# Second layer of a gated MLP by seven products of halves, with each chunk's operations recorded and issued from a written list

## The chip, the cores and the metric

The kernel runs on one core of one Trainium2 chip. The metric is the device time of one launch in microseconds (us). The core's engines work side by side, each through its own queue in order: PE (matrix products; PEld is its load of the stationary operand), DVE (vector), ACT (scalar), POOL (GpSimd) and SP, which here issues nearly all DMAs. SBUF is the on-chip memory, PSUM the accumulators that PE writes.

## The reference

Attention over 8 batches and 8 heads (512 local tokens with a window of 32 and 32 global tokens that see all), then a normalised gated MLP on all 4352 rows of 512 features. Only the MLP is touched by the change.

```python
rms = np.sqrt(np.mean(x * x, axis=-1, keepdims=True) + 1e-06)
xn = x / rms * rms_g
g = xn @ w_gate                      # first layer: 512 -> 1536, twice
silu = g * (1.0 / (1.0 + np.exp(-g)))
val = xn @ w_val
return (silu * val @ w_out)          # second layer: 1536 -> 512
```

## The kernel before

Rows are worked through in nine chunks: chunks 0 to 7 are the batches with 512 local tokens each, chunk 8 holds the 256 global tokens. While PE does the MLP of chunk c, the attention of chunks c+1 and c+2 goes on between its products.

Every fp32 number enters a product as two f16 parts, high and low, so one product is three: high by high, low by high, high by low.

*First layer.* Chunk 0 (order written out in `ORDER`), chunk 1 and chunk 8 use plain products (`moe_in`). Chunks 2 to 7 use `moe_pair`: two of the twelve feature tiles at a time, as a two by two block product done with seven products of halves (numbered 6, 1, 5, 7, 2, 3, 4) instead of eight. Each product is 12 matmuls with 256 moving columns. It needs sums of halves of the operands (`norm_halves` for the activations, `fold` once in chunk 1 for the weights, which go to a DRAM buffer `wd` and are fetched from it by `fetch` for every chunk) and sums of the results (`rest`). Behind it, in steps of a "tail", come the tanh on ACT, two multiplications on DVE (`gate`, `inner`), the high part as an ACT copy (`high`) and the low part as a subtraction, on POOL as a rule (`low`).

*Second layer.* `moe_block`: for each 128 tokens one PSUM bank, 12 feature tiles of three matmuls with 512 moving columns (the weights `wo`, held in SBUF); the stationary operand is the activation. So 36 matmuls a block, 144 a chunk of 512 tokens, 72 in chunk 8. The result is scaled by `inv_k` on ACT or DVE and stored by SP.

*Order.* After chunk 0 a loop over `work` issues one step (a product and its `rest`) at a time; behind each, `slot` issues those attention steps whose distances in steps from the ones they depend on have been kept, `norm_sums`, `norm_all`, `norm_halves` run at fixed distances from the chunk's end, `ch["tail", g]` at fixed places, and `feed` fetches the next weight tile from a list `ring`. Tiles of the pool `wf` (12 buffers of 512 KB) hold fetched weights `wt` and the fp32 sums `s`, `u`, `v`; the pools `wo` (7) and `h` (6) hold the second layer's weights and activations. PSUM banks: `po` twice, `pg`, `pv`, and four `pa` for attention.

The lines named below: L1106 is the first layer's matmul in `moe_pair`, L1264 the second layer's in `moe_block`, L1203 the plain first layer's, L706 and L660 attention's, L1160 `inner`, L157 a subtraction on POOL, L1138 the sum `s(6) + s(1)` on POOL, L1277 and L1275 the results on DVE and ACT, L1083 the fetch, L637 the division of the attention weights on POOL, L1054 and L1063 sums and high parts of `fold`.

Of the kernel before, what the change touches and what calls it, by code (L numbers as in the profile page):

```python
# [22 lines left out]
P = 128  # L23
# [40 lines left out]


@with_exitstack
def attention_moe_kernel(
# [29 lines left out]
    NORM[B - 1] = (17, 15, 12, 7)  # L97
    UNIT = {2: (0, 20), 3: (-26, 2, 12)}
    FOLD = (0, 6, 12, 18, 24, 30, 38, 46, 54)
    ST = 6  # L100
# [119 lines left out]
    def gain_bound():  # L220
        nc.vector.tensor_reduce(g2[:, 0:1], gp[0][:, 0:2], axis=AX.X, op=ALU.max)
        nc.vector.tensor_scalar(g2[:, 1:2], g2[:, 0:1], ginv, float(DM), ALU.mult, ALU.mult)
        nc.vector.tensor_scalar(x2, g2[:, 1:2], ginv, 2.0**-16, ALU.mult, ALU.mult)

# [189 lines left out]
    def out_scale():  # L414
        power(gp[0], 1, 15, k_o)
# [158 lines left out]
    def local_halves(c, b, hp, xt):  # L574
# [58 lines left out]
        def divide(x, bk):  # L633
            e = st["e", x, bk]
            r = st["sm"][:, 2, 8 * x + 4 * bk : 8 * x + 4 * bk + 4]
            nc.vector.reciprocal(r, r)  # L636
            nc.gpsimd.tensor_tensor(e, e, r.unsqueeze(2).to_broadcast([P, 4, P]), ALU.mult)  # L637

# [401 lines left out]
    ]  # L1040

    def fold(f):

        st = {}

        def sums():
            t = [
                pool.tile([P, 1152], F32, tag="st", bufs=ST, name=f"wq{f}")[:, :1024],
                pool.tile([P, 1024], F32, tag="wo", bufs=7, name=f"ws{f}"),
            ]  # L1050
            a, s = (x.rearrange("p (q n) -> p q n", q=4) for x in t)
            nc.vector.tensor_tensor(t[0], wf[f][:, 0, :], wf[f][:, 1, :], ALU.add)
            nc.vector.tensor_tensor(s[:, 1], a[:, 2], a[:, 3], ALU.add)
            nc.vector.tensor_tensor(s[:, 0], s[:, 1], a[:, 0], ALU.subtract)  # L1054
            nc.vector.tensor_tensor(s[:, 2], a[:, 0], a[:, 2], ALU.subtract)
            nc.vector.tensor_tensor(s[:, 3], a[:, 1], s[:, 0], ALU.subtract)
            st["s"] = s
            d = t[0].bitcast(F16)
            st["d"] = d.rearrange("p (q a n) -> p q a n", q=4, a=2)

        def high():
            d = st["d"]
            nc.scalar.copy(d[:, :, 0, :], st["s"])  # L1063
# [21 lines left out]

    def moe_pair(ch, g):

# [38 lines left out]
        def rest(p):  # L1126
# [5 lines left out]
            elif p == 1:  # L1132
                t = pool.tile([P, 1024], F32, tag="wf", bufs=NF, name=f"s1_{g}")
                st["s", 1], st["s", 5] = t[:, :512], t[:, 512:]
                nc.scalar.copy(s(1), st["ps", 1])  # L1135
            elif p == 5:
                nc.vector.tensor_tensor(s(5), st["ps", 5], s(1), ALU.add)  # L1137
                nc.gpsimd.tensor_tensor(s(6), s(6), s(1), ALU.add)  # L1138
            elif p == 7:
# [30 lines left out]
        def low(j, on="P"):  # L1170
            sub(on, st["h"][:, j, 1, :], st["t", j], st["h"][:, j, 0, :])

        ch["tail", g] = [
            lambda: gate(0),
            lambda: (gate(1), inner(0)),
            lambda: (inner(1), high(0)),
            lambda: (high(1), low(0)),
            lambda: low(1),
        ]
        if g == NF // 2 - 1:  # L1180
            ch["tail", g] = [
                lambda: (gate(0), gate(1)),
                lambda: (inner(0), inner(1), high(0)),
                lambda: (high(1), low(0)),
                lambda: low(1, "V"),
                lambda: None,
            ]
# [3 lines left out]
        ]  # L1191


    def moe_in(ch, w, f, n, ps, ks):
# [22 lines left out]

    def moe_f(ch, f, n, on):
        ps = {}
# [9 lines left out]
        def gate():  # L1229
# [6 lines left out]
            later(1, onto)  # L1236

        def inner():
            t = ps["t"]
# [12 lines left out]
            (lambda: half(1, 0), None),  # L1252
            (lambda: half(1, 1), inner),
        ]
# [105 lines left out]
    for c in range(NCH):  # L1360
# [3 lines left out]
        for i, un in enumerate(units):  # L1364
# [6 lines left out]
            for name, fn, pe, after in steps:  # L1371
                st = {"name": name, "fn": fn, "pe": pe, "c": c, "x": xi, "after": [], "at": None}
                st["from"] = (FIRST if c == EARLY else UNIT[len(units)])[i]
                for dep, gap in after:
# [11 lines left out]

    clock = [0]
    base = {}

# [14 lines left out]
    def slot(most, last):  # L1404

        done = 0
        for st in list(todo[:40]):
            if st["c"] > last:
                break
            if st["pe"] and done >= most:  # L1410
                continue
            if ready(st):
                issue(st)
                done += st["pe"]
# [24 lines left out]
    for name in ORDER.split():  # L1439
        job.pop(name)()  # L1440
    stores = [steps[3] for f, steps in folds.items() if f"J{f}" not in job]
    folds = {f: steps for f, steps in folds.items() if f"J{f}" in job}
    row = SL
    left = list(folds.values())
    ring = [(c, g, i) for c in range(EARLY, B) for g in range(NF // 2) for i in range(4)]
    ring += [(B, g, i) for g in range(NF // 2) for i in range(2)]

    def feed():
        if ring:
            fetch(*ring.pop(0))  # L1450

    base[1] = 0
    for c in range(1, NCH):
        n = width[c]
        ch = chunks[c]
        if EARLY <= c < B:
            work = [w for g in range(NF // 2) for w in moe_pair(ch, g)]
        else:
            work = [w for f in range(NF) for w in moe_f(ch, f, n, "P")]
        first = len(work)  # L1460
        work += [w for j in range(n // P) for w in moe_block(ch, j, row)]
        total = len(work)
        base[c + 1] = clock[0] + total
        gaps = NORM.get(c, NORMS)
# [3 lines left out]
        if c + 1 < NCH:  # L1468
# [5 lines left out]
            if not last:  # L1474
                for i, fns in norm_halves(chunks[c + 1], c + 1).items():
                    at[total - gaps[3] + i] = lambda fns=fns: [fn() for fn in fns]
        for k, (products, rest) in enumerate(work):
            products()
            if c + 1 < NCH:
                slot(1, c + 2)  # L1480
                if k == norm_at - 1:
                    assert not chunks[c + 1]["left"]
                    if last:
                        chunks[B]["x"] = [xg[:, kk, :] for kk in range(NK)]
                if k in at:
                    at[k]()
            if rest:
# [4 lines left out]
            if EARLY <= c < B and k >= 7 and k % 7 < 5 and k <= first + 4:  # L1492
                ch["tail", k // 7 - 1][k % 7]()
            if c == 1:
                if k == 1:
# [6 lines left out]
                if 42 <= k < 50:  # L1502
                    feed()
            elif c < B and k < first and k % 7 in (1, 3, 5, 6):
                feed()
            elif c == B - 1 and first <= k < first + 8:
                feed()
        row += n


# [124 lines left out]
```

## Time and profile before

| | |
|---|---|
| median of three runs | 928.01 us (926.51 to 928.34) |
| the profiled execution's own time | 924.96 us |
| its span, first to last instruction | 922.7 us |
| PE busy | 890.3 us, 96% |
| DVE busy | 634.3 us, 69% |
| ACT busy | 495.6 us, 54% |
| POOL busy | 253.5 us, 27% |
| moved by DMA | 173.39 MB, q1 at 56% of 16 engines |

The span is what the trace covers; the execution's own time is 2.3 us longer. Busy time of PE is the union of its matmuls, whose ends are modelled; since matmuls overlap in the array, the pace of a stream is read from a stretch of the chain (so many matmuls in so many us), and not from the duration of one.

### The profile page before, as it was taken

Reading aid. Unit: us, or ns where it says so; the run is one execution under the profiler, and the core shown is the slowest. Engines: PE = TensorE matmul, PEld = TensorE weight load, DVE = VectorE, ACT = ScalarE, POOL = GpSimd, SP = SyncE. Lnnn points to the kernel's source line nnn. Section 1 sums busy time; section 2 is a strip of 40 time slices with the busy share of each in tenths; the row PEclk is TensorE's granted clock in tenths of the full one; section 3 lists DMA queues with packets and bytes.
Section 4 is the critical chain, followed back from the end, with each engine's and each line's share of the span. In section 5 each row is a group of like instructions: output and inputs, shape, how many; then the busy total and the mean of one; then the engine's idle time right before and its main releaser. Section 6 shows DMA issues by size and latency. Waiting matters only on the chain.

```text
span 922.7 us, 26018 instructions
## 1 busy us (share of the span) xinstructions
PE 890.3 (96%) x10836; PEld 608.4 (66%) x10836; DVE 634.3 (69%) x1603; ACT 495.6 (54%) x1232; POOL 253.5 (27%) x219
## 2 busy tenths in 40 slices
PE   5699989999999999999999999999999999999998
PEld 4444446545447885688658874788568865886584
DVE  6999998887796578468765678457846874664331
ACT  6989996545444564357345545356435732553130
POOL 0000000142423252335333353225233431332020
PEclk9799999999999999999999999999999999999999
DMA  9983515686557863495519671776349522796000
GB/s 346 403 305 97 189 47 184 210 258 209 181 189 212 273 202 133 141 297 184 188 48 305 207 246 37 211 262 201 135 139 295 185 93 93 247 273 231 35 1 23
DMA packets 83493, 173.39 MB, mean 188 GB/s; under 512 B 6704, under 2 KB 25392, under 8 KB 83376
## 3 DMA queue, kind: packets, MB, share of 16 engines
q1 hardware_dynamic: 82944, 171.40, 56.0%
q8 instruction: 85, 1.39, 0.6%
q10 hardware_dynamic: 432, 0.33, 0.1%
q14 instruction: 32, 0.26, 0.1%
HBM read 150.21 MB, written 21.50 MB: 186 GB/s over the span
## 4 chain that ended last, share of the span: by engine, by line
PE 84%; DVE 1%; ACT 1%; issue 0%; DVEq 0%
PE pq L1106 36%; PE po L1264 25%; PE p L1203 9%; PE po L1331 3%; PE a L706 3%; PE s L660 3%; PE ga L836 1%; PE gs L779 1%; PE gt L822 1%; ACT e L622 1%; PE t L518 0%; PE s L474 0%; PE a L532 0%; DVE e L488 0%; ACT wq L295 0%
## 5 line engine op out<-in xcount | busy, mean ns | idle before, releaser
L1106 PEld LDWEIGHTS <-wt 128*128 128x128 f16 x3024 | 292.6, 98 | 41.1 <-issue 4.8
L1264 PE MATMUL po<-wo,h 128*128 128x512 f16 x1080 | 236.2, 379 | 0.0
L1106 PE MATMUL pq<-xh,wt 128*128 128x256 f16 x1152 | 204.5, 273 | 0.1
L1264 PEld LDWEIGHTS <-h 128*128 128x128 f16 x1080 | 105.2, 98 | 123.9 <-issue 1.0
L1106 PE MATMUL pq<-xl,wt 128*128 128x256 f16 x576 | 157.1, 273 | 0.7 <-issue 0.7
L1106 PE MATMUL pq<-ht,wt 128*128 128x256 f16 x1296 | 155.4, 273 | 0.0
L637 POOL TENSOR_TENSOR e<-e,sm 128x512 f32<-128x512 f32 x48 | 49.9, 1040 | 291.0 <-DVE sm L636 287.9
L157 POOL TENSOR_TENSOR h<-t,h 128x512 f16<-128x512 f32 (+1 forms) x90 | 102.5, 1146 | 93.1 <-ACT h L1246 52.4
L1203 PE MATMUL p<-xh,wf 128*128 128x512 f16 x384 | 117.6, 379 | 3.4 <-DVE t L1300 1.5
L1203 PEld LDWEIGHTS <-wf 128*128 128x128 f16 x576 | 55.3, 98 | 71.1 <-issue 4.9
L1138 POOL TENSOR_TENSOR s<-s,s 128x512 f32<-128x512 f32 x36 | 47.9, 1331 | 183.3 <-ACT s L1135 111.5
L622 ACT ACTIVATE e<-e,sm 128x128 f32<-128x128 f32 x192 | 75.2, 393 | 37.9 <-DVE sm L608 37.8
L1168 ACT CAST h<-t 128x512 f16<-128x512 f32 x72 | 44.4, 616 | 58.9 <-DVE t L1160 58.3
L1203 PE MATMUL p<-xl,wf 128*128 128x512 f16 x192 | 72.8, 379 | 0.3 <-DVE xl L902 0.3
L1160 DVE SCALAR_TENSOR_TENSOR t<-t,c_h,v 128x512 f32<-128x512 f32 x72 | 71.6, 1001 | 0.0
L1149 ACT ACTIVATE t<-u,half_inv 128x512 f32<-128x512 f32 x72 | 48.0, 714 | 36.9 <-DVE u L1124 28.5
L1124 DVE TENSOR_TENSOR v<-pq,s 128x512 f32<-128x512 f32 x72 | 49.6, 689 | 23.6 <-PE pq L1106 22.8
L1137 DVE TENSOR_TENSOR s<-pq,s 128x512 f32<-128x512 f32 x36 | 24.9, 691 | 46.9 <-PE pq L1106 40.5
L1156 DVE SCALAR_TENSOR_TENSOR t<-t,u 128x512 f32<-128x512 f32 x72 | 47.5, 688 | 1.0 <-ACT t L1149 1.0
L1124 DVE TENSOR_TENSOR u<-pq,s 128x512 f32<-128x512 f32 x36 | 24.9, 691 | 33.6 <-PE pq L1106 25.5
L608 DVE CUSTOM_DVE_ANT_0 e<-s,maskb 128x128 f32<-128x128 f32 x192 | 45.8, 278 | 2.0 <-PE s L660 2.0
L1131 ACT COPY s<-pq 128x512 f32<-128x512 f32 x36 | 21.0, 583 | 46.6 <-PE pq L1106 46.5
(346 smaller groups left out, 1275.5 us busy)
## 6 DMA issues: line engine op xcount, KB each, us to landing
wt<-wd SPq DMA_DIRECT2D x120, 512.0 KB, 4.7
wr<-in_w_in_dram SPq DMA_DIRECT2D x24, 512.0 KB, 8.8
k<-in_qkb_dram SPq DMA_DIRECT2D x24, 448.0 KB, 6.1
gkq<-in_gkq_dram SPq DMA_DIRECT2D x16, 576.0 KB, 6.3
wt<-wd SPq DMA_DIRECT2D x36, 256.0 KB, 4.5
out_dram<-o SPq DMA_DIRECT2D x34, 256.0 KB, 2.0
v<-in_vb_dram SPq DMA_DIRECT2D x24, 352.0 KB, 7.3
v<-in_vw_dram SPq DMA_DIRECT2D x16, 512.0 KB, 8.4
```

The lines of the kernel that those rows point to most:

```text
L157: nc.gpsimd.tensor_tensor(dst, a, b, ALU.subtract)
L608: nc.vector.tensor_tensor_reduce(out=e[:, g, :], in0=ps[:, g * P : (g + 1) * P], in1=late["mask"][:, m * P : (m + 1) * P], scale=-0.125, s ...
L622: nc.scalar.activation(e[:, g, :], e[:, g, :], AF.Exp, bias=sm[:, 0, j + g : j + g + 1], scale=-1.0, accum_out=sm[:, 1, j + g : j + g + 1],)
L637: nc.gpsimd.tensor_tensor(e, e, r.unsqueeze(2).to_broadcast([P, 4, P]), ALU.mult)
L1106: nc.tensor.matmul(ps[:, j * HT : (j + 1) * HT], w[:, j, i, k * P : (k + 1) * P], x[:, k * HT : (k + 1) * HT], start=first, stop=(p in end ...
L1124: nc.vector.tensor_tensor(o, ps, x.rearrange("p (j n) -> p j n", j=2), ALU.add)
L1138: nc.gpsimd.tensor_tensor(s(6), s(6), s(1), ALU.add)
L1149: nc.scalar.activation(t, st["u"][:, j, :], AF.Tanh, scale=half_inv[:, f : f + 1])
L1156: nc.vector.scalar_tensor_tensor(t, t, 1.0, u, ALU.add, ALU.mult)
L1160: nc.vector.scalar_tensor_tensor(t, t, c_h[:, f : f + 1], st["v"][:, j, :], ALU.mult, ALU.mult)
L1203: nc.tensor.matmul(ps[:, :n], rows[:, a, o : o + P], ch[z][k][:, :n], start=(k == 0 and i == 0), stop=(k == NK - 1 and i == 2),)
L1264: nc.tensor.matmul(ps[0], ch["h", f][:, a, j * P : (j + 1) * P], wo[f][:, z, :], start=(f == 0 and q == 0), stop=(f == NF - 1 and q == 2),)
```

## The change

In chunks 3 to 8 the second layer also becomes a two by two block product by seven products of halves: token halves by output halves, feature tile by feature tile pair. Chunk 2 keeps `moe_block`.

- `fold_out` (new, in chunk 2, six times): sums of quarters of `wo` (two POOL additions, four DVE subtractions), split in high (ACT) and low (POOL), and stored with the plain quarters to two DRAM buffers `wa` and `wb` (five DMAs).
- `fetch_out` (new): 11 tiles of 512 KB (one of them half full) per chunk from `wa` and `wb` into the pool `wf`.
- `moe_out` (new) in place of `moe_block`: 42 blocks (product p, pair g), each of 6 matmuls with 256 moving columns (3 in chunk 8), written two to a step. Products 1, 5, 6 come pair by pair, then 2, 7, 3, 4. Results: product 1 and 6 are scaled on ACT, 5 is added on DVE, one sum on POOL, then 2 on ACT, 7, 3, 4 on DVE; two stores a chunk instead of four.
- `out_parts` (new) in place of `high` and `low`: `formed` writes the product into `v` (as `inner` did into `t`), four DVE operations form sums of halves, the halves and the sums get high parts (two ACT copies of 128x1024) and low parts (on POOL 128x512 and 128x256 for the halves, two of 128x512 for the sums; for the last pair of a chunk the latter two are on DVE).
- `s(6) + s(1)` moves from POOL to DVE, reading PSUM.
- The division of the attention weights in chunks 5 to 7 moves from one POOL operation of 128x512 to four ACT operations of 128x128.
- Scales change by powers of two.
- The order: what the loop issues after chunk 0 is recorded under names, and written in the order of a list per chunk (`ORDERS`; chunks 3, 4 and 5 share one). `P` is a product step, `R` its results, `t` the tail, `n` the normalisation, `w` a fetch, `O` a block of the second layer, and names such as `S/0+2.0` are attention steps (step S of unit 0, two chunks ahead). The lead of the fetches is now a time in steps (`LEAD`).

```diff
+_ORDER_3 = """
+Y/0+1.1 P1.0 L/2+1.0 P0.0 R0.0 Y/0+1.0 P7.0 Y/0+1.2 R1.1 GS/1+1.0 GM/1+1.0 GN/1+1.0 R1.0 P2.0 R2.0
...
+X/2+1.3 w32.0 P40.0 R40.0 R41.0 w31.0 P41.0 R41.2 S/0+2.0 t42.0 R41.1 N2/0+2.0 M2/0+2.0 M1/0+2.0
+w34.0 w60.0 t42.1 t43.1 O0.0 O3.0 Y/2+1.2 N0/0+2.0 Y/2+1.3 E2/0+2.0 O1.0 O4.0 O7.0 N1/0+2.0 O2.0
+O5.0 w44.0 n42.0 t39.0 t40.0 E1/0+2.0 O6.0 t43.0 t44.4 t45.2 w36.0 O9.0 O10.0 w46.0 F1/0+2.0 t44.0
+t44.2 t44.1 O12.0 t45.1 N3/0+2.0 O13.0 GL/1+2.0 O8.0 O11.0 O14.0 t44.3 n42.1 n44.0 w40.0 w50.0 t40.1
+M0/0+2.0 t45.0 t46.0 O17.0 F2/0+2.0 E0/0+2.0 R50.0 t38.3 O16.0 F0/0+2.0 O15.0 n44.1 M3/0+2.0
...
+ORDERS = {1: _ORDER_1, 2: _ORDER_2, 3: _ORDER_3, 4: _ORDER_3, 5: _ORDER_3, 6: _ORDER_6, 7: _ORDER_7, 8: _ORDER_8}
...
+            if c > EARLY + 2:
+                for g in range(4):
+                    nc.scalar.mul(e[:, g, :], e[:, g, :], r[:, g : g + 1])
+            else:
+                nc.gpsimd.tensor_tensor(e, e, r.unsqueeze(2).to_broadcast([P, 4, P]), ALU.mult)
...
+    BLOCKS = [(p, g) for g in range(NF // 2) for p in ALONG]
+    BLOCKS += [(p, g) for p in AFTER for g in range(NF // 2)]
...
+                if parts:
+                    nc.vector.tensor_tensor(s(6), st["ps", 1], s(6), ALU.add)
...
+                nc.vector.tensor_tensor(s[:, 0, 0], v[:, 0, 1], v[:, 1, 1], ALU.add)
+                nc.vector.tensor_tensor(s[:, 1, 0], v[:, 0, 0], v[:, 0, 1], ALU.subtract)
...
+                nc.vector.tensor_tensor(s[:, 0, 1], s[:, 0, 0], v[:, 0, 0], ALU.subtract)
+                nc.vector.tensor_tensor(s[:, 1, 1], v[:, 1, 0], s[:, 0, 1], ALU.subtract)
...
+                sub(on, lo[:, :, :w], v[:, :, :w], hi[:, :, :w])
+                sub(on, lo[:, 1, w:], v[:, 1, w:], hi[:, 1, w:])
...
+                for j in range(2):
+                    sub(on, lo[:, j], s[:, j], hi[:, j])
...
+                for j in range(nj):
+                    for a, x in ((0, hi), (0, lo), (1, hi)):
+                        nc.tensor.matmul(
+                            ps[:, j * HT : (j + 1) * HT],
+                            x[:, j * P : (j + 1) * P],
+                            u[:, a, :],
...
-            work = [w for g in range(NF // 2) for w in moe_pair(ch, g)]
+            work = [w for g in range(NF // 2) for w in moe_pair(ch, g, c > EARLY)]
...
+        if c > EARLY:
+            work += moe_out(ch, c, n, row)
+        else:
+            work += [w for j in range(n // P) for w in moe_block(ch, j, row)]
...
+    orders = {c: names.split() for c, names in ORDERS.items()}
+    for c, plan in plans.items():
+        for name in orders.get(c, plan):
+            for call in plan.pop(name) if c in orders else plan[name]:
+                call()
```

More of the change, by code (lines that the diff above doesn't have):

```diff
@@ L1171, in low, with formed @@
             sub(on, st["h"][:, j, 1, :], st["t", j], st["h"][:, j, 0, :])
+        def formed(j):
+            f, v = 2 * g + j, st["v"][:, j, :]
+            nc.vector.scalar_tensor_tensor(
+                v, st["t", j], c_h[:, f : f + 1], v, ALU.mult, ALU.mult
+            )
+        sums, units, splits = out_parts(ch, g, lambda: (st["v"], st["u"]), SL)
         ch["tail", g] = [
@@ L1252, in moe_f @@
             (lambda: half(1, 0), None),
-            (lambda: half(1, 1), inner),
+            (lambda: half(1, 1), formed if c == B else inner),
         ]
@@ L1387, in attention_moe_kernel @@
     clock = [0]
+    now_in = [1]
     base = {}
@@ L1481, in attention_moe_kernel @@
                 if k == norm_at - 1:
-                    assert not chunks[c + 1]["left"]
+                    assert not chunks[c + 1]["left"], [
+                        (st["name"], st["c"]) for st in todo if st["c"] == c + 1
+                    ]
                     if last:
```

420 lines of the change are left out of this document (401 added, 19 removed).

## The prediction, made before the changed kernel had run

> **What bounds the kernel now.** First the page's busy times and slices: they say which engine is full, and when.
>
> ```profile
> PE 890.3 (96%) x10836; PEld 608.4 (66%) x10836; DVE 634.3 (69%) x1603; ACT 495.6 (54%) x1232; POOL 253.5 (27%) x219
> PE   5699989999999999999999999999999999999998
> PEclk9799999999999999999999999999999999999999
> ```
>
> PE is full from the eighth slice on, at full granted clock. Second, the waits of PE alone, in 247 to 922 us and in 167 to 247 us:
>
> ```profile
> PE pq L1106 <- issue: 0.7, 1, 0.7
> PE s L660 <- issue: 1.5, 1, 1.5
> ```
>
> Two gaps, 2.2 us, in three quarters of the kernel. So behind 167 us (chunks 1 to 8) a microsecond of PE work taken out is a microsecond gained, as long as nothing else becomes late. Third, the chain that ended last in order of time (start, us, what), which gives the pace of each kind of product:
>
> ```profile
> 417.74 20.96 PE pq L1106 x192
> ...
> 754.74 23.32 PE po L1264 x108
> ...
> 871.79 31.44 PE p L1203 x288
> 903.23 15.55 PE po L1264 x72
> ```
>
> A matmul with 512 moving columns takes 23.32/108 = 215.9 ns in a stream (15.55/72 = 216.0 in chunk 8); one with 256 takes 20.96/192 = 109.2 ns (31.44/288 = 109.2). Half the columns cost half the time, though each has its own 128x128 load. Fourth, the stages of one chunk (first layer, second layer) and whole chunks; columns are the stretch, its us, then busy us of PE, PEld, DVE, ACT and POOL with their counts, the clock, the DMA share and GB/s:
>
> ```profile
> 280.00:347.00 67.00, 66.89 (x1078) 58.21 (x1077) 42.09 (x100) 36.15 (x93) 27.28 (x23) 1.00 0.76 241
> 347.00:381.80 34.80, 34.80 (x356) 17.17 (x354) 27.53 (x76) 15.48 (x51) 11.46 (x9) 1.00 0.23 88
> 381.80:446.70 64.90, 64.90 (x996) 56.82 (x997) 39.53 (x96) 35.95 (x90) 26.04 (x22) 1.00 0.76 245
> 446.70:482.00 35.30, 35.30 (x360) 17.66 (x359) 27.54 (x76) 15.46 (x51) 11.46 (x9) 1.00 0.24 90
> 582.00:682.00 100.00, 100.00 (x1354) 74.17 (x1352) 67.05 (x172) 51.40 (x140) 37.51 (x31) 1.00 0.58 189
> ```
>
> A chunk is 100 us of PE without a hole. DVE is next, 67 us, and denser in the second layer's stage (27.54 of 35.30, 78%) than in the first's (61%).
>
> **PE's term.** Second layer of chunks 3 to 7, each: out go 144 x 215.9 = 31.09 us, in come 7 products x 6 pairs x 6 matmuls = 252 x 109.2 = 27.52 us: -3.57, five times -17.9. Chunk 8: 72 x 216 = 15.55 out, 126 x 109.2 = 13.76 in: -1.8. Together **-19.7 us**. The pace is the unknown. The new matmul has the first layer's form (128x128 f16 stationary, 256 moving), whose worst stage is this row, by line L1106:
>
> ```profile
> 381.80:446.70 64.90, 56.44 (x504) 48.64 (x504) 1.00 0.76 245
> ```
>
> 56.44/504 = 112.0 ns, with what its changes to attention and back cost in it. At 112.0 the term is 5 x (28.22 - 31.09) + (14.11 - 15.55) = -15.8. I take 109.2, since interruptions are there before as well; -15.8 is the other end.
>
> **What comes on the other engines.** These groups (busy, mean ns) give the prices:
>
> ```profile
> L1160 DVE SCALAR_TENSOR_TENSOR t<-t,c_h,v 128x512 f32<-128x512 f32 x72 | 71.6, 1001 | 0.0
> L1303 DVE SCALAR_TENSOR_TENSOR t<-t,c_h,p 128x512 f32<-128x512 f32 x12 | 9.0, 749 | 0.0
> L1156 DVE SCALAR_TENSOR_TENSOR t<-t,u 128x512 f32<-128x512 f32 x72 | 47.5, 688 | 1.0 <-ACT t L1149 1.0
> L1054 DVE TENSOR_TENSOR ws<-ws,wq 128x256 f32<-128x256 f32 x12 | 5.1, 425 | 0.4
> L1277 DVE TENSOR_SCALAR o<-po,kk 128x512 f32<-128x512 f32 x15 | 11.2, 745 | 47.5 <-PE po L1264 47.5
> L1168 ACT CAST h<-t 128x512 f16<-128x512 f32 x72 | 44.4, 616 | 58.9 <-DVE t L1160 58.3
> L1063 ACT CAST wq<-ws 128x1024 f16<-128x1024 f32 x12 | 12.5, 1039 | 4.4 <-DVE ws L1056 4.2
> L1275 ACT ACTIVATE o<-po,kk 128x512 f32<-128x512 f32 x15 | 10.2, 681 | 29.0 <-PE po L1264 29.0
> L718 ACT COPY x<-a 128x256 f32<-128x256 f32 x24 | 8.7, 363 | 12.6 <-PE a L706 12.6
> L157 POOL TENSOR_TENSOR h<-t,h 128x512 f16<-128x512 f32 x78 | 94.5, 1220 | 60.0 <-ACT h L1168 40.7 <-ACT h L1246 19.3
> L637 POOL TENSOR_TENSOR e<-e,sm 128x512 f32<-128x512 f32 x48 | 49.9, 1040 | 291.0 <-DVE sm L636 287.9 <-DMA wt<-wd 3.1
> L1138 POOL TENSOR_TENSOR s<-s,s 128x512 f32<-128x512 f32 x36 | 47.9, 1331 | 183.3 <-ACT s L1135 111.5 <-issue 71.7
> ```
>
> DVE, per chunk 3 to 7: 24 sums x 0.425 = 10.2; `s(6)` from PSUM 6 x about 0.69 (L1156's size) = 4.1; the last pair's low parts 0.7 more; results 4 x 0.745 for 2 x 0.745 = 1.5; `formed` costs what `inner` did. +16.5: from 67.05 to 83.6 of 100.0 - 3.6 = 96.4 us, 87%. ACT: high parts 12 x 1.039 for 12 x 0.616 = +5.1, results 3 for 2 = +0.7: 57. In chunks 5 to 7 the division adds 32 copies of 128x128, at most L718's 0.363 each and at least half of it: 5.8 to 11.6, so 63 to 69 of 96. POOL: out 11 x 1.22 and 6 x 1.33 = 21.4; in 6 x (1.22 + about half of it) + 10 x 1.22 + 1.33 = 24.5; +3.1, so 40.6, and from chunk 5 on less 8 x 1.04 = 8.3. All three stay below PE's 96.4: the cover is there on the mean, and I count these at nothing except at the two places below.
>
> Chunk 2 pays for `fold_out`: POOL 6 x (2 + 2) x 1.22 = 29 on 27.28 + 11.46 = 38.7, to 68 of 102 us; DVE 6 x 4 x 0.425 = 10.2 on 69.6; ACT 6 x 1.04. Nobody on PE waits for it before chunk 3, so it is counted at nothing; uncovered, DVE's 10.2 would be its price.
>
> **DMA and SP's queue.** `wa` and `wb` hold (18 + 24) x 128 KB = 5.5 MB: written once by 30 DMAs, read six times by 66, of 512 KB. The first layer's stage already runs at 245 GB/s, the second's at 90; chunk 3 moved 245 x 64.9 + 90 x 35.3 = 19.1 MB, and with 5.5 more over 96.4 us it is 255 GB/s on the mean. The page's GB/s row has slices of 346 and 403, so the bandwidth holds. What can be late is a single fetch:
>
> ```profile
> wt<-wd SPq DMA_DIRECT2D x120, 512.0 KB, 4.7
> SPq L1083 <- PE pq L1106: 177.7, 66, 6.0
> SPq L1278 <- ACT o L1275: 129.6, 14, 38.8
> ```
>
> SP issues in order. A fetch waits for its buffer (177.7 us behind PE), and a store that waits for its result (up to 38.8 us) holds all fetches behind it. The 12 buffers of `wf` now serve 48 + 11 + 4 tiles a chunk instead of 48, and `u`, `v` live some four steps longer, until the last low part is made. A lead of 9 steps is 9 x 12 x 0.109 = 11.8 us against 4.7 to land: about 7 us of slack. Counted at nothing; without cover it is the third rival.
>
> **Where PE can wait.** (a) The last pair of a chunk: its result must become six operands while PE has only the other pairs' blocks. From the list for chunks 3 to 5: behind P41 PE has scores and then 15 blocks, 15 x 6 x 0.109 = 9.8 us, before O17 (the last pair). DVE has in that order the result (0.69), a gate (0.69), attention's M and N behind the scores, the other gate (0.69), `formed` twice (0.75 each), three sums, one more sum, M and N again, then the low part (0.7), with one ACT copy of 1.04 between the last sum and it.
>
> ```profile
> 455.90 1.99 PE s L660 x127
> ...
> 457.79 0.25 DVE L608 CUSTOM_DVE_ANT_0 e<-s,maskb 128x128 f32<-128x128 f32 x1
> 451.22 0.70 DVE L940 STREAM_TRANSPOSE st<-sq 128x512 f32<-128x512 f32 x1
> ```
>
> The score products are 1.99 us of PE, so cover is 11.8. DVE: 0.69 + 3 x 0.5 of M and N (two of about 0.25 each), 2 x 0.69, 2 x 0.75, N twice 1.0, transpose 0.70, sums 4 x 0.425, N 0.5, the reduction 0.7, then the ACT copy 1.04, and 0.7: 11.4, and some 0.1 of hand-over at each of the engine changes: about 12.3. A wait of 0.5, in each of six chunks: +3.0. (b) The start of the next chunk. DVE in the second layer's stage: 27.54 + last pair's sums 1.7 + 0.7 + results 1.5 = 31.4 of 35.30 - 3.57 = 31.7 us, 99%. The list lets P1 go ahead of P0 and moves score work to later, so I take a quarter of a microsecond in five chunks, +1.2; the ends are 0 (all moved) and 2 each (one operand late by a few DVE operations). (c) The two gaps of 2.2 us stand at places that the lists reorder; I take half, -1.1, ends 0 and -2.2.
>
> Sum: -19.7 + 3.0 + 1.2 - 1.1 = **-16.6 us**. Against the profiled execution's 924.96 (span 922.7 and 2.3 around it; 3 us below the median) that is 908.4, against the median of 928.01 it is **911.4**.
>
> **A rule against it.** Row: the DVE product with both operands in SBUF (L1160) takes 1001 ns, with one in PSUM (L1303) 749; in the chunk above, one that started at 448.87 took 2.42 for two while POOL ran from 448.62:
>
> ```profile
> 448.62 1.46 POOL L723 TENSOR_TENSOR sq<-sq,sq 128x512 f32<-128x512 f32 x1 [2.23 <-ACT sq L721]
> 448.87 2.42 DVE L1160 SCALAR_TENSOR_TENSOR t<-t,c_h,v 128x512 f32<-128x512 f32 x2
> ```
>
> That is 0.25 us more on the mean. The Trainium skill (SBUF — State Buffer, "Who interferes with whom") says that a DVE instruction with two SBUF inputs and a GpSimd instruction that reads SBUF exclude one another, whoever starts first. The 24 new sums are of this kind; by that rule each would pay about the same, and L1054's 0.425 (while POOL did little) would be too low. In rows: 24 x 0.25 = 6.0 us, DVE 89.6 of 96.4, and 32.4 of 31.7 in the second layer's stage.
>
> **Rivals.** *DVE sets the pace* (the paragraph above, from rows alone): the stage overflows and PE waits some 2 us at each of (a) and (b) in chunks 3 to 7 instead of 0.75: -19.7 + 5 x 4 + 0.5 at most, of which attention's freedom gives back about half: -10, **918**, up to 925. For it: 99%. Against: the whole chunk has 7 to 13 us of DVE left. *Slower: a fetch is late.* SP stands behind a store or a buffer not yet free, at one place in each chunk, for one landing time: 6 x 4.7 = 28.2, so +8.5, **936**. It decides from 19.7/6 = 3.3 us a chunk. For it: 63 tiles through 12 buffers, an in-order queue. Against: 7 us of slack, bandwidth. *The change doesn't do what it says*: the 256-column product not at half price. The rows of two stages say 109.2; even 112.0 gives -15.8 and leaves it faster. To cancel the gain it would have to be 31.09/252 = 123 ns: **928**.
>
> **How the numbers follow.** Forecast (905 to 916) 0.70; DVE's pace (916 to 925) 0.18; other cases near no change 0.04; a late fetch, slower, 0.08. About 0.2% (1.9 us) is what a measurement of this kernel tells from no change. Faster 0.89, same 0.03, slower 0.08. Low end: 928.0 - 19.7 - 2.2 and a microsecond of scatter (the lowest run is 1.5 below the median) = 905. High end: into DVE's case, 922; above it are a fifth of that case, the late fetch and half of the cases near no change, and little lies below 905.
>
> **What would show it.** Right: the new matmuls at 109 ns in the chain, 252 in about 27.5 us; a chunk period of 96 to 97 us in place of 100; waits of PE behind 167 us of 3 to 6 us, in front of the last pair's blocks; DVE at 84 to 90 us a chunk. Wrong: waits of PE on a sum or a low part at the chunk's start, above 2 us each (DVE); waits of PE on `wu` or `wt` DMAs (the queue); chunk 2 longer than 102 us (`fold_out`).

## The result, and the profile after

The changed kernel takes 956.04 us (949.95 to 956.34, four executions) against 927.65 for the kernel before in the same series: a ratio of 1.0292, interval 1.0249 to 1.0334. It is slower by 28 us where 16.6 were to be gained. Below, the profiled execution of 956.05 us (span 954.2) is read against that of the kernel before (924.96, span 922.7); the spans differ by 31.5 us. After chunk 0's order and part of chunk 1, nearly all instructions are issued from one line, L1870 (the recorder's call), so rows are told apart by their tiles: `pr` is a product of the new second layer, `pq` one of the first, `hu` and `hs` the operands made of halves and of sums, `wt` and `wu` the fetched weights.

The page's busy times and DMA queues:

```profile
PE 884.8 (93%) x11430; PEld 674.0 (71%) x11430; DVE 729.2 (76%) x1831; ACT 558.2 (58%) x1341; POOL 274.5 (29%) x244
...
q1 hardware_dynamic: 100448, 209.94, 66.5%
q8 instruction: 89, 1.46, 0.6%
```

DVE rose by 94.9 us and is still at 76%. PE's work shrank, and its share fell from 96% to 93%: PE stands idle. How much, from the windows of PE and the others behind 167 us (columns as before), first of the kernel before:

```profile
167.00:918.00 751.00, 748.56 (x9136) 527.84 (x9134) 483.44 (x1178) 353.98 (x926) 253.27 (x215) 1.00 0.56 182
```

and of the changed kernel:

```profile
167.00:950.00 783.00, 740.04 (x9728) 588.78 (x9727) 578.27 (x1406) 415.77 (x1035) 274.26 (x240) 0.99 0.69 224
```

PE is idle for 783.00 - 740.04 = 43.0 us instead of 2.4: 40.5 more. Its busy time fell by 8.5 only, at a mean clock of 0.99. The waits of PE in 167 to 954 us (waited for; us, times, longest) say what it stood for:

```profile
PE pq L1870 <- DMA wt<-wd: 16.4, 12, 4.3
PE pr L1870 <- DMA wu<-wa: 8.4, 3, 4.0
PE s L1870 <- issue: 5.5, 4, 4.2
PE pr L1870 <- POOL hs L1870: 3.9, 1, 3.9
PE pq L1870 <- DVE ht L1870: 2.6, 1, 2.6
PE gs L1870 <- DMA gkq<-in_gkq_dram: 2.3, 4, 0.9
PE a L1870 <- issue: 1.9, 2, 1.0
...
PE pr L1870 <- DMA wu<-wb: 0.6, 1, 0.6
PE p L1870 <- DMA wt<-wd: 0.5, 1, 0.5
```

Transfers are 28.2 us of it (16.4 + 8.4 + 2.3 + 0.6 + 0.5). The 2.6 on `ht` are an operand of the first layer, at chunk 3's start. The 3.9 on `hs` stand in the wrong row: the matmul behind that wait loads `hu`, and the last low part of a `hu` that POOL made ahead of it was done at 562.7 us, five microseconds before the wait began. First the row of POOL, then that of PE:

```profile
561.56 1.16 POOL L1870 TENSOR_TENSOR hu<-v,hu 128x512 f16<-128x512 f32 x1 [4.92 <-ACT hu L1870]
...
571.78 1.25 PE L1870 MATMUL pr<-wu,hu 128*128 128x256 f16 x5 [3.89 <-POOL hs L1870]
```

With one pool of buffers (below) a wait of 4.4 us stands at the same instruction, there under `issue`. So this one is counted with `issue`, which is then 11.3 us (5.5 + 1.9 + 3.9). The chain that ended last shows how one fetch came to be late:

```profile
521.03 1.28 DVE u L1870
...
522.34 1.05 ACT hs L1870
...
523.46 3.40 POOL hs L1870 x3
526.86 0.02 issue
526.88 6.33 DMA wt<-wd
...
533.25 2.77 PE pq L1870 x16
...
582.75 15.73 PE pr L1870 x144
```

A sum in `u`, its high part on ACT, three low parts on POOL; only then is the buffer free, SP's fetch goes out 0.02 us later, lands after 6.33 us, and PE starts. For every late fetch the trace has the semaphore that SP waited for ahead of it. Seven of the twelve waits on `wt`, 12.3 of the 16.4 us, are for fetches that went out like this one, when POOL had made the last low part from `u` or `v`. The two long waits on `wu` (3.6 and 4.0) are of another kind. Their buffers were freed by a product in its usual course, 6 us before PE stopped, and the transfers, issued behind attention's loads `gkq` and `gv`, took 9.7 and 10.0 us. The chain around the second, and a window of it, in which the DMA engines were busy all the time (share 1.03):

```profile
672.62 4.05 PE pr L1870 x36
676.68 10.00 DMA wu<-wa
686.72 7.74 PE pr L1870 x54
```

```profile
682.00:687.00 5.00, 0.95 (x11) 0.81 (x9) 3.30 (x20) 0.48 (x3) 0.82 (x1) 1.00 1.03 318
```

So two things make a fetch late: a buffer that comes free late, and a landing longer than the 4.7 us of before. SP's own waits, for all that it issues:

```profile
SPq L1870 <- PE pq L1870: 107.5, 48, 6.1
SPq L1870 <- PE pr L1870: 80.9, 28, 9.7
SPq L1870 <- DVE u L1870: 56.3, 22, 7.5
...
SPq L1870 <- POOL hs L1870: 26.6, 12, 6.0
SPq L1870 <- DVE v L1870: 24.5, 20, 3.2
```

The row on POOL is new: `hs` 26.6 us and (not shown) `hu` 13.9, where the kernel before has none of that size. `u` and `v` are names of first-layer results as well; the kernel before had such waits on DVE as `t` (51.9 and 17.8 us) and `u` (8.4), so these two rows are not all new. The last row of the first chain above says that the products themselves keep the pace that was forecast: 15.73/144 = 109.2 ns.

The rest is the clock. A window behind the wait of 4.0 us:

```profile
687.00:690.00 3.00, 3.00 (x20) 2.25 (x19) 0.00 (x0) 2.34 (x11) 0.00 (x0) 0.62 0.65 246
```

The granted clock is 0.62 in it, and 20 matmuls in 3.00 us of busy PE are 150 ns each on the mean. In the trace's clock records there are six stretches of 3.41 us at half clock between 167 us and the end, each starting within 1.1 us of PE's resuming from a gap of 2.2 to 4.3 us; in the kernel before there are none while PE works. Half of PE's busy time in them, 9.8 us, is lost. So the 32.0 us by which the two windows differ are 40.5 of waits, 9.8 of clock, and -18.3 of work at full clock (740.04 - 9.8 - 748.56).

### The profile page after: what moved, and what is told of

It is laid out like the page before. It is cut to its first block, busy times and chain, and to the rows that moved or that the text cites. A ratio compares the mean times of both kernels' runs of the same rounds, so it can differ in the third digit from the quotient of the medians.

```text
span 954.2 us, 27731 instructions
## 1 busy us (share of the span) xinstructions
PE 884.8 (93%) x11430; PEld 674.0 (71%) x11430; DVE 729.2 (76%) x1831; ACT 558.2 (58%) x1341; POOL 274.5 (29%) x244
## 3 DMA queue, kind: packets, MB, share of 16 engines
q1 hardware_dynamic: 100448, 209.94, 66.5%
## 4 chain that ended last, share of the span: by engine, by line
PE 40%; issue 9%; DMA 9%; POOL 4%; DVE 4%; ACT 1%; SPq 0%; POOLq 0%; DVEq 0%; ACTq 0%
PE pq L1870 20%; PE pr L1870 12%; DMA wt<-wd 5%; PE p L1870 3%; POOL hs L1870 3%; DMA wu<-wa 3%; PE po L1870 2%; PE s L1870 1%; PE a L1870 1%; POOL hu L1870 1%; DVE x L1870 1%; DMA gv<-in_gv_dram 1%; DMA wu<-wb 1%; ACT hs L1870 1%; DVE h L1870 0%
## 5 line engine op out<-in xcount | busy, mean ns | idle before, releaser
L1870 PEld LDWEIGHTS <-wt 128*128 128x128 f16 x3312 | 323.4, 99 | 68.6 <-DMA wt<-wd 20.4
L1870 PE MATMUL pq<-xh,wt 128*128 128x256 f16 x1152 | 206.8, 274 | 6.7 <-DMA wt<-wd 6.2
L1870 PE MATMUL pq<-ht,wt 128*128 128x256 f16 x1296 | 159.4, 276 | 12.9 <-DMA wt<-wd 10.3
L1870 PE MATMUL pq<-xl,wt 128*128 128x256 f16 x576 | 157.8, 274 | 0.0
L1870 ACT ACTIVATE e<-e,sm 128x128 f32<-128x128 f32 x288 | 104.5, 391 | 20.0 <-DVE sm L1870 19.7
L1870 POOL TENSOR_TENSOR hu<-v,hu 128x256 f16<-128x256 f32 (+1 forms) x60 | 58.5, 989 | 199.3 <-ACT hu L1870 199.3
L1870 PE MATMUL pr<-wu,hs 128*128 128x256 f16 x792 | 95.2, 276 | 7.7 <-DMA wu<-wa 7.7
L1870 POOL TENSOR_TENSOR e<-e,sm 128x512 f32<-128x512 f32 x24 | 28.1, 1181 | 222.4 <-DVE sm L1870 222.1
L1870 PEld LDWEIGHTS <-hs 128*128 128x128 f16 x792 | 78.6, 100 | 18.0 <-DVE nt L1870 7.9
L1870 PE MATMUL pr<-wu,hu 128*128 128x256 f16 x594 | 72.1, 275 | 5.2 <-POOL hs L1870 3.9
L1870 DVE TENSOR_TENSOR s<-pq,s 128x512 f32<-128x512 f32 x66 | 45.3, 686 | 35.0 <-ACT s L1870 21.0
L1870 POOL TENSOR_TENSOR hs<-u,hs 128x512 f16<-128x512 f32 x50 | 59.5, 1206 | 43.2 <-ACT hs L1870 42.3
L1870 ACT COPY s<-pq 128x512 f32<-128x512 f32 x72 | 41.3, 582 | 50.6 <-PE pq L1870 44.1
L1870 PEld LDWEIGHTS <-hu 128*128 128x128 f16 x594 | 58.2, 99 | 13.7 <-POOL hs L1870 4.2
L1870 PE MATMUL po<-wo,h 128*128 128x512 f16 x288 | 64.5, 385 | 0.0
L1870 DVE TENSOR_TENSOR v<-pq,s 128x512 f32<-128x512 f32 x72 | 49.4, 687 | 17.2 <-PE pq L1870 16.0
L1870 DVE SCALAR_TENSOR_TENSOR t<-t,u 128x512 f32<-128x512 f32 x72 | 54.8, 770 | 8.7 <-ACT t L1870 8.3
L1870 ACT ACTIVATE t<-u,half_inv 128x512 f32<-128x512 f32 x72 | 49.2, 717 | 17.4 <-DVE u L1870 14.9
L1870 PE MATMUL p<-xh,wf 128*128 128x512 f16 x192 | 58.6, 379 | 0.0
L1870 PEld LDWEIGHTS <-h 128*128 128x128 f16 x288 | 28.3, 100 | 34.5 <-issue 2.5
```

The lines of the kernel that those rows point to most:

```text
L1870: return lambda *a, **k: write(self.engine, lambda: call(*a, **k))
```

## The experiments

The reading to be tested: buffers that come free late make fetches late, and PE's waits for them bring the clock down. The first rival: the lists, searched for other durations than these, are at fault.

**The lists: `recorded`, `recorded12`, `listed12`.** `recorded` is the changed kernel with the operations in the order in which they are recorded:

```diff
-ORDERS = {1: _ORDER_1, 2: _ORDER_2, 3: _ORDER_3, 4: _ORDER_3, 5: _ORDER_3, 6: _ORDER_6, 7: _ORDER_7, 8: _ORDER_8}
+ORDERS = {}
```

> The seven-product second layer as changed, but every chunk in the order in which it is recorded, no list. Buffers (fetches wait for one of the 12 wf buffers, which the longer life of u and v frees late): the same operations and the same 12 buffers, so waits of PE on wt and wu stay, 940 to 965 us. The lists (they were ordered by durations that do not hold, so that fetches stand in SP's queue out of the order of use and late): without them most of the 26 us of waits on wt and wu and the 10 us of halved clock go, 908 to 925. DVE and POOL too full: no order helps, 945 to 965.

1001.68 us (998.31 to 1003.08), ratio 1.0815 (1.0791 to 1.0839). Its waits of PE:

```profile
PE pq L1870 <- DVE s L1870: 17.6, 22, 2.1
PE pr L1870 <- ACT os L1870: 14.5, 3, 4.8
```

`recorded12` keeps the lists of chunks 3 to 8 alone, `listed12` those of chunks 1 and 2 alone.

> Lists only for chunks 3 to 8, chunks 1 and 2 as recorded. Chunk 2 took 114.7 us from its first product to chunk 3's against 101.4 before. If chunks 1's and 2's lists did that, about 9 us less than the changed kernel: 943 to 948. If fold_out in chunk 2 did it, no change: 952 to 960.

> Lists only for chunks 1 and 2, chunks 3 to 8 as recorded. The lists: chunks 3 to 8 lose their late fetches, 920 to 930. Buffers or full engines: 945 to 965.

968.87 and 998.61 us (one execution each). All three kernels lie above every range that was expected for them. The lists are worth 45 us, 33 to 43 of them in chunks 3 to 8 (1001.68 - 968.87, 998.61 - 956.04): leaving them out makes the kernel slower still. That the waits on `wt` would stay without the lists was wrong too: in `recorded` there are none. The likely reason, argued and not tested, is that PE is held back there by operands (DVE and ACT) for so long that every fetch is in time. No list made for the durations measured here was tried, so it stays open whether another order of all operations would have kept the gain with 12 buffers.

**What holds the buffers: `tiny_low`.** The low parts of the sums are made for 32 of 256 columns, and the products read the high part in their place:

```diff
-                    sub(on, lo[:, j], s[:, j], hi[:, j])
+                    sub(on, lo[:, j, :32], s[:, j, :32], hi[:, j, :32])
```

> All lists kept. The low parts of the sums are formed for an eighth of their columns only, and the products of those sums read the high part twice (so the result leaves those low parts out): POOL loses about 2.1 us per pair and u is free about 2 us earlier. Buffers freed late through POOL: waits on wt and wu fall by half or more, 930 to 942. The lists (position of fetches and SP's order): little, 946 to 955. Engines too full (POOL): 930 to 940.

941.44 us (one execution), in the range that was expected if POOL frees the buffers late. `wt` falls from 16.4 to 9.5 us, `wu` from 9.0 to 6.4, less than the half that was expected. A part of the lateness hangs on POOL's last low part, as the chain showed; not all.

**The order of the fetches: `use_order`.** In chunks 3 to 8 the names `w...` are put in the order in which PE uses the tiles, as early as 12 buffers allow.

> The lists of chunks 3 to 8 with the fetches alone moved: they stand in the order in which PE uses them, each as early as 12 buffers allow and at most 16 us of PE work ahead; every other engine's order is kept. In the lists as given a fetch such as chunk 4's wt for pair 3, last tile, stands before those of pair 1 and 2. SP's order (a fetch that is not yet needed holds a buffer and stands ahead of one that is): the 26 us of waits on wt and wu and most of the 10 us of halved clock go, 918 to 930. Buffers freed late by DVE and POOL: the fetches wait as before, 945 to 958.

968.64 us, ratio 1.0447 (1.0403 to 1.0490), above both ranges. PE hardly waits for `wt` any more (0.4 us), but for attention's loads, which stand behind the fetches in SP's queue:

```profile
PE gs L2026 <- DMA gkq<-in_gkq_dram: 14.5, 6, 7.8
PE ga L2026 <- DMA gv<-in_gv_dram: 13.7, 5, 4.7
```

In this order the lateness has only moved to other transfers; that no order could remove it with 12 buffers and one queue is not shown.

**More buffers for the fetches: `one_pool`.** The pools `wf` (12), `wo` (7) and `h` (6), whose tiles have one size, become one of 25; the lists and the bytes stay.

```diff
-    BUFS = {"wf": NF, "wo": 7, "h": NF // 2}
+    BUFS = {"wf": 25}
...
-        t = pool.tile([P, 2, 2, 2, HT], F16, tag="wf", bufs=NF, name=f"wt{c}_{g}{i}")
+        t = pool.tile([P, 2, 2, 2, HT], F16, tag="wf", bufs=25, name=f"wt{c}_{g}{i}")
...
-                hi, lo = st["u"] = both("hu", "wo", 7)
+                hi, lo = st["u"] = both("hu", "wf", 25)
```

> The changed kernel with the pools wf, wo and h (12, 7 and 6 buffers of 4 KB a partition) made one pool of 25, same bytes, same lists. At the start of a chunk the 13 of wo and h are idle. Buffers: waits on wt and wu mostly go, 920 to 932. SP's order alone: the wrong order stays, 940 to 955. DVE and ACT as the bound: 940 to 955.

One execution of 926.89 us. Its largest waits of PE:

```profile
PE s L1870 <- issue: 8.6, 5, 4.7
PE pq L1870 <- DMA wt<-wd: 3.1, 2, 2.6
...
PE gs L1870 <- DMA gkq<-in_gkq_dram: 1.8, 1, 1.8
PE pr L1870 <- DMA wu<-wa: 1.6, 2, 0.9
```

Six more executions were taken in a further series:

> The changed kernel with the pools wf, wo and h as one pool of 25 buffers, timed against the kernel before. If the buffers that came free late were all of the loss beyond the halved clock and the seven products' gain were left whole, it would lie below the kernel before by over 0.2% (920 us or less). If what remains (waits behind no data, under the higher DMA load, some 12 us, and two or three stretches at half clock) eats the gain of 19.7 us, it lies within 0.5% of the kernel before, 922 to 930 us, as the single run at 926.89 says.

936.43 us (932.02 to 941.34), ratio 1.0098 (1.0077 to 1.0119), above both ranges: the single execution was a lucky one. The fetches are in time again (28.2 us of waits on transfers have become 6.5 in the first profile and 5.0 in this one), the time falls by 20 us, and yet the kernel stays behind the one before. What grew is a wait for nothing that the profile shows (here in an execution of 941.34 us):

```profile
PE s L1870 <- issue: 12.6, 6, 4.7
PE pr L1870 <- issue: 4.4, 1, 4.4
PE pq L1870 <- DMA wt<-wd: 2.6, 1, 2.6
```

`one_pool_use_order` joins the two edits. Its fetches of weights never hold PE, and the waits for `issue` are there all the same (`s` 11.8, `pr` 4.5): 935.92 us, ratio 1.0097 (1.0060 to 1.0133). The time is in the range of "DVE and ACT set the pace", but PE does not wait on them, so neither expectation fits.

> Both: one pool of 25 and the fetches in the order of use, at most 16 us ahead. Fetch theories, either of them: no waits on wt and wu are left; what is left is chunk 2 (13 us longer than before), the last pair of each chunk and the results, 912 to 926. If DVE and ACT set the pace: 935 or more, with waits of PE on them in place of those on DMA.

`before_one_pool` has the one pool in the kernel before: 931.31 us (one execution, against 925.69 in its series), above the range that was expected. Fetches that run further ahead do not help a kernel whose fetches were in time; `s <- issue` is 5.2 us there, in four waits, against 1.5.

> The kernel before with its pools wf, wo and h made one of 25. PE never waited there for a fetch (waits behind 167 us: 2.2 us), so every theory of the buffers says no change: 924 to 928.

**Fewer bytes: `half_fetch_12`, `half_fetch_one_pool`.** In chunks 3 to 8 only half of each weight tile is fetched, and the products read that half twice.

```diff
-        nc.sync.dma_start(t[:, :n], src)
+        nc.sync.dma_start(t[:, :2], src[:, :2])
```

> The changed kernel (12, 7 and 6 buffers, its lists) with half of every fetched tile of chunks 3 to 8: 256 KB instead of 512, and the products read that half twice, so the result is that of other weights. Buffers and waits on SP stay. Buffers freed late are the cause: a fetch lands about 1 us earlier (256 KB took 4.5 us, 512 KB 5.3), so of 26 us of waits on wt and wu a quarter to a third goes, 940 to 950. The DMA engines' load is the cause: most of it goes, 920 to 932.

> The same half tiles in the kernel with one pool of 25 buffers, where 21.7 us of waits of PE are left behind 165 us, 12 of them filed under issue inside the short attention products. If those are the instruction stream held up by the DMA load, they fall to about 3 as before the change, and 926.9 goes to 912 to 918. If DVE's lateness or something else is behind them: 922 to 927.

932.5 us with 12 buffers, 915.27 with one pool (one execution each). With 12 buffers the waits on transfers fall from 28.2 to 8.4 us. That is close to what was expected if the load of the DMA engines is the cause (920 to 932), and not what was expected of the buffers alone (940 to 950): a fetch of 256 KB lands in 3.4 us here, one of 512 KB took 5.3. A buffer freed late costs PE time because a long landing follows it; more buffers, or fewer bytes, each take most of the lateness away. The windows of the kernel with one pool:

```profile
167.00:910.00 743.00, 730.10 (x9731) 586.12 (x9728) 577.88 (x1406) 415.20 (x1035) 274.55 (x240) 1.00 0.57 178
```

PE is busy for 730.10 us, 18.5 less than in the kernel before, and idle for 12.9. With the transfers out of the way by both edits, the same operations end 10.4 us below the kernel before in their series (925.69), where 16.6 were forecast. Of the 12.9 us, 2.6 are the wait on `ht` and 7.8 are waits of the kind that the part on `issue` below counts.

**`fold_out` and chunk 2: `no_fold`, `one_pool_fold_last`.** From its first product to that of the next, chunk 2 takes 110.6 us instead of 101.5 (times of the products in the trace). `no_fold` leaves `fold_out` away and lets `wu` be read from `wd`; `one_pool_fold_last` puts its last pair behind chunk 3's normalisation.

> fold_out is left out of chunk 2 (no sums of wo, no stores; the fetches of wu read the first layer's weights, so the result is that of other weights). All lists kept. If fold_out makes chunk 2 longer (114.7 us from its first product to chunk 3's, 101.4 before): 8 to 13 us less, 943 to 948. If the list of chunk 2 does: no change, 950 to 957.

> One pool of 25, and in chunk 2's list fold_out's last pair (POOL, DVE, ACT and its stores) moved behind the normalisation for chunk 3. PE waited 2.6 us for chunk 3's ht there, and the clock fell to half for 3.4 us behind it. If DVE's queue at that place is the cause: 4 us less, 922 to 924, and the wait on ht is gone. If the shared access of DVE and POOL is it: the ht operations keep their 2.6 us and it stays at 926 to 928.

957.23 us (one execution), chunk 2 still 110.2: no cost of `fold_out` is seen, as predicted. What makes chunk 2 longer by 9.1 us in the changed kernel's trace are 6.1 us of waits, 4.2 of them one wait for `issue`, 1.7 us of half clock, and 80 products of attention more than before, some 1.5 us. In `one_pool_fold_last` the wait of 2.6 us on `ht` at chunk 3's start is gone, and others came (`gs <- DVE x` 2.4): 934.52 us, ratio 1.0087 (1.0066 to 1.0108), above both ranges and about that of `one_pool`.

**Load without late buffers: `before_load`, `before_load_one`.** The kernel before, with 28 MB of further transfers that nobody waits for:

```diff
+            if EARLY < c < B and first <= k < first + 22 and (k - first) % 2 == 0:
+                i = (k - first) // 2
+                src = wd[i % 6][:, 0:2].rearrange("p a b c n -> p (a b c n)")
+                nc.sync.dma_start(more[:, i].rearrange("p a b n -> p (a b n)"), src)
```

> The kernel before, with 11 more transfers of 512 KB in the second layer's stage of each of the chunks 3 to 7 (28 MB in all), from the folded weights to a DRAM buffer that nobody reads; no buffer of SBUF is used for them and no instruction of PE, DVE, ACT or POOL is added. Theory 'buffers': the fetches were late because their buffers came free late, and the load alone does nothing: within 0.3% of the kernel before. Theory 'load': the transfers delay others in the rings: PE waits for the next 256 instructions of its own stream (waits for 'issue' that recur every 256 instructions) or for wt, 5 us or more in all, 0.5% or more slower.

> The same added transfers in the kernel before with its pools wf, wo and h as one pool, so that the fetches run further ahead. If the waits for PE's own instructions come from how many transfers stand in the rings at once, this is slower than either edit alone (more than 931 us and more than the kernel with the added transfers alone); if not, it lies at the slower of the two.

927.39 us, ratio 1.0024 (1.0002 to 1.0045), and 928.55, ratio 1.0028 (1.0013 to 1.0042). The second layer's stage of `before_load`, 88 GB/s before:

```profile
447.00:482.00 35.00, 35.00 (x306) 17.34 (x311) 27.87 (x77) 15.96 (x51) 12.41 (x10) 1.00 0.77 264
```

```profile
PE s L660 <- issue: 3.6, 3, 2.3
```

Over the whole span the packets on q1 take 64.9% of the DMA engines' time, against 66.5% after the change, and PE works on. So busy DMA engines alone are not the cause. But the added transfers hardly delay the fetches (512 KB land in 4.9 us instead of 4.7), so the runs do not show what the long landings of the changed kernel would do to this one. `before_load_one` is not slower than the slower of the two edits alone, so the number of transfers under way does not by itself bring waits for `issue`.

**What "issue" is: `one_pool_spread`, `spread`.** The page's queue row has 89 instruction packets for 11430 matmuls and 11430 loads, one for every 257. If all that PE executes is numbered in the order of the starts, its waits on semaphores included, then in every run of this document all waits for `issue` of more than 0.6 us behind 167 us stand a multiple of 256 apart, the two gaps of the kernel before among them. A packet on q8 ends 1.2 to 1.8 us ahead of each resumption: PE waits for its next instructions. The 3.9 us filed under `hs` stand at such a place too, 1.3 us behind a packet. All waits at these places are 2.2 us in the kernel before, 11.3 after the change, 12.2 and 21.0 in the two profiles with one pool. Most are in front of or inside attention's short products, and the lists have put those together: with PE's waits taken out, 256 matmuls and loads leave within 3.2 us at 24 places (12 in the kernel before), 512 within 6.4 us at 3 (none). The two kernels put a product of the MLP between the two halves of attention's values (`A`, `B`) and ahead of the scores (`S`):

```diff
-A/2+1.0 R39.0 t35.0 R34.2 t36.0 B/2+1.0
...
-X/2+1.3 w32.0 P40.0 R40.0 R41.0 w31.0 P41.0 R41.2 S/0+2.0 t42.0 R41.1 N2/0+2.0 M2/0+2.0 M1/0+2.0
+A/2+1.0 R39.0 t35.0 R34.2 t36.0 t35.1 t36.1
...
+t37.1 t37.0 t38.0 t38.1 t31.3 t37.2 t38.2 w32.0 P40.0 R40.0 R41.0 w31.0 P41.0 B/2+1.0 Y/2+1.0
...
+Y/2+1.3 O1.0 O4.0 S/0+2.0 N2/0+2.0 M2/0+2.0 M1/0+2.0 N0/0+2.0 E2/0+2.0 O7.0 N1/0+2.0 O2.0 O5.0 w44.0
```

> The changed kernel with one pool of 25 buffers, and the lists of chunks 2 to 6 edited so that a product of the MLP (24 matmuls as a rule) stands between the two halves of attention's values (A and B) and ahead of the scores (S), which the lists had put back to back. The same instructions, the same transfers in the same order. Theory 'instruction stream': PE's waits at the end of each 256 of its instructions (23.9 us in the one pool's last profile, 13.9 in its first) come from short products issued back to back, 512 instructions in 6 us, faster than the next ones arrive; spread out, these waits fall to 8 us or less and the time to 915 to 928 us. Rival: they come from the transfers that run ahead, wherever the short products stand: the waits stay at 14 us or more and the time at 932 us or more.

> The same edit of the lists in the changed kernel itself (12 buffers). The waits at the end of 256 instructions are 14.3 us of its 49 us of gaps: by the theory of the instruction stream some 8 to 10 us go and the waits on wt and wu stay (944 to 950 us); by the rival nothing changes (952 us or more).

940.42 us (935.60 to 946.42), ratio 1.0154 (1.0104 to 1.0203), and 955.16, ratio 1.0336 (1.0275 to 1.0397). In `one_pool_spread` no 512 leave within 6.4 us any more, and the waits for instructions are 10.3 us, against 12.2 and 21.0 (13.9 and 23.9 in the expectation, which counted otherwise); but the operands that were moved with `B` and `S` are late now:

```profile
PE s L1870 <- issue: 6.2, 3, 3.5
PE pr L1870 <- issue: 3.3, 2, 2.2
...
PE po L1870 <- ACT h L1870: 1.5, 1, 1.5
PE po L1870 <- DVE v L1870: 1.5, 1, 1.5
PE pq L1870 <- DVE v L1870: 1.3, 1, 1.3
```

Neither expectation held: the waits fell by less than the one said, and the time did not fall. In `spread` they went from 11.3 to 4.8 us and `wu` from 9.0 to 3.1, `wt` rose to 18.3, and the time stayed. That PE waits for instructions is seen, and that spreading the short products out lowers the wait. That the bunching alone makes it is not settled, since with half the bytes, one pool and the same lists it is less too (7.8 us).

## Why the prediction was wrong

**The step that failed** is the one headed "DMA and SP's queue": "A lead of 9 steps is 9 x 12 x 0.109 = 11.8 us against 4.7 to land: about 7 us of slack. Counted at nothing". The lead in the list is when a fetch may stand in the order, not when its buffer is free. With 63 tiles through 12 buffers, of which `u` and `v` hold theirs until the last low part, fetches went out as buffers came free (0.02 us later in the chain above), with 6.33 us still to land. The other side of the comparison, 4.7 us to land, failed as well: the two long waits on `wu` had 6 us of reserve and landings of 9.7 and 10.0. Counted at 0, the waits on transfers came to 28.2 us, of which 12.3 lie behind a last low part and 7.7 behind these two landings. More buffers took most of it away (`one_pool`), and so did fewer bytes (`half_fetch_12`). The rival "a fetch is late" had the mechanism and by coincidence the sum (6 x 4.7 = 28.2); it was given 0.08. It was not one place in each chunk: 12 waits on `wt` and 4 on `wu`, of up to 4.3 us. The argument against it, bandwidth, holds on the mean (DMA share 0.69) and not at the waits (1.03 in the window above).

**Missing altogether: the clock.** 9.8 us, beside 43.0 us of waits. A long wait of PE cost more than its length here.

**PE's term.** -19.7 was forecast; 109.2 ns a matmul is measured, and PE's busy time at full clock fell by 18.3. This step was right.

**(a) The last pair.** 0.5 us in each of six chunks, +3.0. No such wait is seen: the one row on `hs` is a wait for instructions. What the chain of operations would have cost without the other waits stays open.

**(b) The next chunk's start.** +1.2; measured 2.6 on `ht` once and 0.5 on `s`, 3.1.

**(c) The gaps that were there.** Forecast -1.1; the waits for instructions went from 2.2 to 11.3, +9.1. That a list could make new ones was not thought of.

**Other engines.** DVE, forecast at 84 to 90 us a chunk, is at 729.2 us in all, 94.9 more, of which five chunks at +16.5 and chunk 2's 10.2 make 92.7. It does not set the pace: beside `ht`, PE's waits on DVE and POOL are 0.5 us, so the second rival falls. These engines count through the buffers that they free late. The rule on shared access named there is seen at single instructions, first on DVE, then on POOL:

```profile
518.43 0.42 DVE L1870 TENSOR_TENSOR u<-u,v 128x256 f32<-128x256 f32 x1
...
520.94 1.36 DVE L1870 TENSOR_TENSOR u<-v 128x256 f32<-128x256 f32 x1
```

```profile
520.23 1.79 POOL L1870 TENSOR_TENSOR hu<-v,hu 128x256 f16<-128x256 f32 x2 [5.03 <-ACT hu L1870]
```

The sum that meets POOL's low part takes 1.36 us instead of 0.42, and it stands in the chain of the late fetch above. Trainium skill, SBUF — State Buffer ("Who interferes with whom"): a DVE instruction with two SBUF inputs and a GpSimd one that reads SBUF shut each other out. The trace agrees: of the 120 such sums, the 97 with POOL idle took at most 0.43 us, and of the 23 beside a POOL operation 11 took 0.51 to 1.36. It is not a price on each: the 120 paid 4.8 us in all, 0.04 each, where 0.25 had been put on each.

**The lists** were taken as neutral; they are worth 45 us, and the change would be slower by 8% without them.

No version of the changed kernel that does the whole work beats the kernel before. The nearest have one pool of buffers and end 0.9 to 1.0% above it.

## What to carry to other kernels

A fetch has as much slack as its buffer has been free, not as the lead in the order says: count, for each buffer, who reads it last and how long ahead of the next use that is, and set it against the landing time under the new load. A change that takes work from a full engine and adds buffers' lifetimes and fetches turns a compute bound into a late transfer, and bandwidth on the mean says nothing of it. Single executions of a kernel with many short waits scatter by 10 us and more (926.89 and 932 to 941 for one kernel); sign and size need a series.

## What the hardware showed that was not expected

PE's clock falls to half for 3.41 us behind waits of 2.2 to 4.3 us, most of it after PE has resumed; behind one wait of 3.6 us (470.96 to 474.60) it did not. The clock records tell why. The half-clock stretches start on a fixed grid of 3.41 us, and what counts is PE's idle time within one interval of the grid. In this trace all six intervals with 2.19 us of idle time or more are followed by half clock, and none with 1.89 or less; in the traces of all runs here together, all 71 with 2.02 us or more. The wait of 3.6 us lay across a grid point, 1.75 us on one side and 1.89 on the other. Trainium skill, TensorE: Matmul & The Clock Gate ("What's actually happening"): the gate watches a free-running window of 3413 ns and halves the clock after an idle one. The length and the free run agree; that 2.0 us of idle time in a window were enough here is less than the page's idle window.

A stream of short products can outrun PE's instructions: where 128 matmuls and 128 loads leave in 1.96 us, the next packet of 256 came late, by up to 4.7 us in one such place with one pool and 1.5 us in the kernel before.

The landing time of 512 KB grew with the number of buffers more than with the bytes. It is 4.7 us in the kernel before and 4.9 in `before_load`, with 28 MB more. With one pool of 25 it is 5.8 in the kernel before (`before_one_pool`, the same bytes). After the change it is, first with 12 buffers, then with one pool (`one_pool_timed`):

```profile
wt<-wd SPq DMA_DIRECT2D x120, 512.0 KB, 5.3
```

```profile
wt<-wd SPq DMA_DIRECT2D x120, 512.0 KB, 7.4
```

More buffers made each fetch slower, and PE waited less for it all the same, since it went out earlier.
